# Output projection by token group with all sums formed ahead, residual copies behind the w2 loads, attention portions resized

## The chip, the cores and the metric

The kernel runs on one core of one Trainium2 chip. The metric is the device time of one execution in microseconds (us). It is about 1.7 us longer than the span in the profile, which counts from the first to the last instruction.

The engines are called as in the profile: PE is TensorE (PEld is its weight load), DVE is VectorE, ACT is ScalarE, POOL is GpSimd, SP is SyncE, which issues plain DMAs. "SPq" and "POOLq" are the sequencers that issue DMAs.

## The reference

One sequence of 2048 tokens, width 1024, bf16. A layer norm feeds two branches, and the result joins both with the input.

```python
xn = layernorm(x)
q, k, v = split(xn @ wqkv)                  # 32 heads of 32
# each token attends to 8 positions: itself and every second one before it
logits = q . k[pos - 2*w] * Dh**-0.5, w = 0..7      (masked where pos - 2*w < 0)
s = (softmax(logits) @ v[pos - 2*w]) @ wo            # output projection
g = silu((silu(xn @ w1) * (xn @ w3)) @ w2)           # MLP of inner width 3584
out = x + s * g
```

## The kernel before

Each large product is done with seven block products instead of eight, on two-by-two blocks of both factors: sums of blocks (s1 to s4 of the left factor, t1 to t4 of the right one) are formed on DVE, and products are accumulated in PSUM. For the output projection these are a11·b11, a12·b21, s1·t1, s2·t2, s3·t3, s4·b22 and a22·t4. A product is begun in one PSUM tile, copied by ACT to another where it serves as the start of a second chain, and finished by adding a stored partial result.

PE works through qkv (to about 160 us), the MLP's up and down parts of the first 1024 tokens and of the second, and a projection after each down part (about 505 and 700 us). The attention itself is work for DVE. It is cut in pieces that a generator hands out between the pieces of the foreground:

```python
def att_work():                       # cut: two chunks of 512 tokens at a time
    yield from scores(c, range(W))
    hooks.append(lambda: score_sums(c))
    yield STOP                        # ends the portion: the foreground runs the hook first
    exponents(c)
    yield 3.0                         # what the piece is booked at, in us of DVE
    yield from scores(c + 1, [0])
    weights(c)
    yield 2.5
    ...
PACE = (9, 8.8, 7.8, 8, 8.3)          # us of such work per step of the foreground, by stage
```

The projection goes product by product over two groups of 256 tokens (gp = 0, 1). s2 and s4 are formed in the middle of it:

```python
product(pa, a11, b11, True)                        # both groups
pb = [bank2(...) for gp in G2]
for gp in G2:
    act_copy(pb[gp][:], pa[gp][:])                 # ACT
with hp():
    nc.vector.tensor_sub(s2, s1, a11)
product(pa, a12, b21, False, finish(0, 0))         # needs pa free, so after the copy
with hp():
    nc.vector.tensor_sub(s4, a12, s2)
product(pe, s1, t1, True, ...)
product(pb, s2, t2, False, ...)
product(pb, s3, t3, False, finish(1, 1))
product(pe, s4, b22, False, finish(0, 1))
product(pb, a22, t4, False, finish(1, 0))
```

A finished piece s*g is not added to x by an engine. x was copied to the output beforehand (seven plain DMAs of 512 KB, issued between 25 and 35 us), and the piece is added to it by an accumulating DMA from POOL. Only the last 512 x 512 piece is done otherwise, with x loaded on the chip, an addition on DVE and a plain store by SP:

```python
def finished(b, u, dh, gp, ps, add):
    last = b == 1 and (u, dh) == (1, 0)
    ...
        if last:
            for i in I:
                ...
                nc.vector.tensor_add(g[:, i], g[:, i], xw[0][:, gp, i])
                nc.sync.dma_start(out=out_rows(...)[:, i], in_=g[:, i])
            return
        to_bf16(d, ps, add)
        anchor["v"] = nc.vector.tensor_mul(g, d, g)
        nc.gpsimd.dma_start(out=out_rows(out_flat, b, u, dh, gp), in_=g, accum_op=ALU.add)
```

While PE works on k, the weights of v ("wv") are loaded over a buffer that is just coming free, and their four sums are put into DVE's program as soon as the load is issued:

```python
def before_v(g):                  # called after the first and the second of k's two groups
    if g > 0:
        return
    for h in I:
        qkv_load(2, h, wv[h])
    tr(3)
    qkv_sums(*wv, sv)             # s1, s2, s4, s3 of wv
qkv_seven(1, 0, wk0, wk1, sk, before_v, snap[2:4])
```

Of the kernel before, what the change touches and what calls it, by code (L numbers as in the profile page):

```python
# [17 lines left out]
def kernel(  # L18
# [218 lines left out]

    def ln_dve(c, sts):
# [66 lines left out]

    def behind(key):
        return tc.issue_after(anchor[key].ins) if key in anchor else nullcontext()
# [182 lines left out]
    def att_work():  # L490
        for c in range(0, NC, 2):
# [5 lines left out]
            yield 3.0  # L497
            yield from scores(c + 1, [0])
            weights(c)
            yield 2.5  # L500
            yield from scores(c + 1, range(1, W))
            while c == 2 and "wo" not in state:
                yield STOP
            for n, t in enumerate(values(c)):
                yield t
                if n == 3:
                    hooks.append(lambda: score_sums(c + 1))
                    yield STOP
                    exponents(c + 1)
                    yield 3.0  # L510
                elif n == 7:
                    weights(c + 1)
                    yield 2.5
# [16 lines left out]
    PACE = (9, 8.8, 7.8, 8, 8.3)  # L530

    def bg(us):
# [5 lines left out]
        with priority(BG), behind("v"):  # L538
            while pace["credit"] > 0 and not hooks:
# [7 lines left out]
    def drain(c):  # L547
        n = 0
        while c not in state:
            bg(1)  # L550
            n += 1
        if n:
            print("drain", c, n)
# [66 lines left out]
    def mlp_up(b):  # L620
# [8 lines left out]
        for n, (g, fb) in enumerate(work):  # L629
# [32 lines left out]
            def e21(pb, f2=f2, hl=hl, n=n, fb=fb, h=h, g=g, both=both, last=last, m=m):  # L662
# [15 lines left out]
                if both and g == 0:  # L678
                    w2_step()
                    residual()  # L680
# [7 lines left out]
    def w2_load(fb):  # L688
        tiles["t", fb] = slot(4 + fb % 2, (2, 2, CH)) if fb < QB else r4(("t", fb), (2, 2, CH))
        nc.sync.dma_start(out=tiles["t", fb], in_=w2_q[:, fb])  # L690
# [148 lines left out]
    def wo_prepare(b):  # L839
# [5 lines left out]
        free = rows(0, 6)  # L845
        s1 = free[:, 0:4 * CH].bitcast(FP16).rearrange("p (j n) -> p j n", j=4)
        su2 = [free[:, (1 + gp) * 4 * CH:(2 + gp) * 4 * CH].bitcast(FP32).rearrange("p (i n) -> p i n", i=2) for gp in G2]
        a11, a12, a21, a22 = oT[:, 0, 0:4, :], oT[:, 0, 4:8, :], oT[:, 1, 0:4, :], oT[:, 1, 4:8, :]
        s2, s4, s3 = o16[:, 0, 0:4, :], o16[:, 0, 4:8, :], o16[:, 1, 0:4, :]

        wx[b] = (a11, a12, a21, a22, s1, s2, s3, s4), (b11, b12, b21, b22, t1, t2, t3, t4), su2
        with behind("v"):
            nc.vector.tensor_sub(t1, b12, b11)
            nc.vector.tensor_add(s1, a21, a22)
            nc.vector.tensor_sub(t2, b22, t1)
            nc.vector.tensor_sub(s3, a11, a21)
# [4 lines left out]
    def wo(b):  # L861
        def finish(u, dh, gp, ps, add=None):
            finished(b, u, dh, gp, ps, add)

        (a11, a12, a21, a22, s1, s2, s3, s4), (b11, b12, b21, b22, t1, t2, t3, t4), su2 = wx[b]

        def product(ps, lhs, rhs, first, after=None):
            run_hooks()
            for gp in G2:
                for i in I:  # L870
                    g = gp * 2 + i
                    mm(ps[gp][:, i], [lhs[:, j, g * P:(g + 1) * P] for j in range(4)], [rhs[:, j, :] for j in range(4)], first)
                if after is not None:
                    after(gp)

        pa = [bank2(f"wa{b}_{gp}") for gp in G2]
        product(pa, a11, b11, True)
        pb = [bank2(f"wb{b}_{gp}") for gp in G2]
        for gp in G2:
            act_copy(pb[gp][:], pa[gp][:])  # L880
        with hp():
            nc.vector.tensor_sub(s2, s1, a11)
        product(pa, a12, b21, False, lambda gp: finish(0, 0, gp, pa[gp]))
        with hp():
            nc.vector.tensor_sub(s4, a12, s2)
        pe = [bank2(f"we{b}_{gp}") for gp in G2]
        sp5 = [k4(f"wsp{b}_{gp}") for gp in G2]
        bg(7 * (1 - b))
        product(pe, s1, t1, True, lambda gp: act_copy(sp5[gp][:], pe[gp][:]))
        product(pb, s2, t2, False, lambda gp: act_copy(su2[gp], pb[gp][:]))  # L890
        bg(7 * (1 - b))
        product(pb, s3, t3, False, lambda gp: finish(1, 1, gp, pb[gp], sp5[gp][:]))
# [168 lines left out]
```

## Time and profile before

| what | us |
|---|---|
| median of the first 3 runs | 737.1 (736.4 to 737.7) |
| span of the profiled run | 732.3 |
| PE busy | 717.0 (98%) |
| DVE busy | 622.9 (85%) |
| last matmul to the end of the span | 7.0 |

The profile's page of the kernel before: the span, and busy time, share and instruction count of each engine.

```profile
span 732.3 us, 8789 instructions
...
PE 717.0 (98%) x3367; PEld 345.6 (47%) x3367; DVE 622.9 (85%) x676; ACT 314.2 (43%) x326; POOL 106.3 (15%) x161
```

PE bounds the kernel: only 15.3 us of the span are not PE time. A 128x512 matmul starts every 0.216 us, so a gap can be measured as the time from the start of one matmul to the start of the next, less 0.216 us. All gaps quoted below are computed so. The waits view names who ended PE's waits (us in total, times, longest); it counts from the modelled end of a matmul and so reads some 0.15 us lower.

```profile
PE wa L149 <- ACT wb L159: 1.6, 1, 1.6
PE aq L149 <- ACT bq L159: 1.5, 1, 1.5
...
PE bm L149 <- DVE wring L660: 0.8, 2, 0.5
```

These are three places: the first projection at 510 us (gap 1.81), the k products at 67 us (1.69), and two steps of the MLP at 310 and 335 us (0.68 and 0.65, the second in two steps of 0.48 and 0.17). What happened at 510 us is in the timeline of the kernel before (start us, us, engine, line, operation, out<-in, form, count, and in brackets the idle time before it with what ended it):

```profile
505.13 3.62 PE L149 MATMUL wa<-wring,oT 128*128 128x512 bf16 x16
...
507.12 1.22 DVE L438 TENSOR_TENSOR Es<-Es 128x1024 f32<-128x1024 f32 x1
...
508.37 1.06 ACT L440 ACTIVATE Es<-Es 128x1024 f32<-128x1024 f32 x1 [0.72 <-DVE Es L438]
...
509.33 1.91 ACT L159 COPY wb<-wa 128x1024 f32<-128x1024 f32 x2
...
510.39 1.45 PE L149 MATMUL wa<-wring,oT 128*128 128x512 bf16 x6 [1.65 <-ACT wb L159]
```

The copy of the first products to `wb` stood in ACT's order behind an exponential of the attention, which waited for DVE. PE had one product (16 matmuls for two groups) and then needed the copy.

At 67 us, the same view of the kernel before:

```profile
60.44 1.22 DVE L316 TENSOR_TENSOR wring<-wring 128x2048 f16<-128x2048 bf16 x1 [5.33 <-DMA wring<-in_A_wqkv_dram]
...
65.11 1.22 DVE L351 TENSOR_TENSOR pk<-eq,uq 128x1024 bf16<-128x1024 f32 x1
...
66.42 1.00 ACT L159 COPY bq<-aq 128x1024 f32<-128x1024 f32 x1 [6.28 <-DVE pk L351]
...
67.47 1.89 PE L149 MATMUL aq<-xT,wring 128*128 128x512 bf16 x8 [1.53 <-ACT bq L159]
```

DVE stands still for 5.33 us until wv has landed, then forms its four sums (L316 to L319), and only then does the addition L351 for k, whose PSUM tile ACT needs for its copy, for which PE waits.

The tail of the kernel before, in the same view: the last accumulating DMA is issued 0.7 us before PE's last matmul ends (725.31), and the last plain stores after it.

```profile
724.61 1.19 POOL L936 DMA_DIRECT2D out_dram<-h_sb  x1 [0.67 <-DVE h_sb L935]
...
725.20 3.19 SPq L932 DMA_DIRECT2D out_dram<-h_sb  x4
```

### The profile page before, as it was taken

The page shows a single profiled execution, that of the slowest core. Times are in us where ns is not written, and L with a number is a line of the kernel's source. Part 1 is how long each engine was busy: PE and PEld are TensorE (multiplying, and loading weights), DVE is VectorE, ACT ScalarE, POOL GpSimd, SP SyncE. Part 2 cuts the span into 40 slices and gives each one's busy share as a digit, 9 for nine tenths or more (in the row PEclk, how much of TensorE's full clock was granted, in tenths as well). Part 3 has the DMA queues.
Part 4 walks back from the last instruction along what each step waited for, and adds up shares of the span by engine and source line. Part 5 has one row for each costly group of instructions (what it writes and reads, how often), then busy time and mean ns, then how long its engine had stood idle before and what let it go on. Part 6 is the DMA issues. An engine that isn't in the chain of part 4 may idle for free.

```text
span 732.3 us, 8789 instructions
## 1 busy us (share of the span) xinstructions
PE 717.0 (98%) x3367; PEld 345.6 (47%) x3367; DVE 622.9 (85%) x676; ACT 314.2 (43%) x326; POOL 106.3 (15%) x161
## 2 busy tenths in 40 slices
PE   8999999999999999999999999999999999999996
PEld 4655665654444444444444444444444444444442
DVE  8996379886999886998999899959979899999535
ACT  5744343437654546654545411124364663121241
POOL 0000000010130110232302010010533032100012
PEclk9999999999999999999999999999999999999998
DMA  9899448864344343467756664559799364553525
GB/s 336 278 237 331 197 147 285 272 234 155 104 133 139 110 149 94 150 198 219 231 173 226 204 206 149 163 189 374 183 285 319 116 179 138 174 185 125 191 30 86
DMA packets 117577, 140.82 MB, mean 192 GB/s; under 512 B 14240, under 2 KB 91040, under 8 KB 116896
## 3 DMA queue, kind: packets, MB, share of 16 engines
q1 hardware_dynamic: 103408, 100.94, 44.2%
q0 software_dynamic: 14128, 39.33, 17.8%
q8 instruction: 26, 0.43, 0.2%
q14 instruction: 15, 0.12, 0.1%
HBM read 98.30 MB, written 39.32 MB: 188 GB/s over the span
## 4 chain that ended last, share of the span: by engine, by line
PE 83%; DVE 11%; DMA 2%; ACT 1%; issue 1%; SPq 0%; DVEq 0%; ACTq 0%
PE bm L149 17%; PE em L149 11%; PE am L149 11%; PE db L149 10%; PE bq L149 7%; PE de L149 7%; PE da L149 7%; PE eq L149 4%; PE aq L149 4%; PE wb L149 2%; PE wa L149 2%; DMA wring<-in_A_wqkv_dram 2%; PE we L149 1%; DVE BC L465 1%; DVE stats L246 1%
## 5 line engine op out<-in xcount | busy, mean ns | idle before, releaser
L149 PEld LDWEIGHTS <-wring 128*128 128x128 f16 (+1 forms) x1920 | 201.6, 105 | 217.9 <-issue 6.8
L149 PEld LDWEIGHTS <-h_sb 128*128 128x128 f16 (+1 forms) x1024 | 107.8, 106 | 113.7 <-DVE xs L291 1.0
L149 PE MATMUL bm<-xs,wring 128*128 128x512 f16 x504 | 117.4, 379 | 0.1
L149 PE MATMUL am<-xT,wring 128*128 128x512 bf16 x336 | 79.9, 379 | 0.1
L410 DVE TENSOR_TENSOR pt<-qt,kT 128x4096 bf16<-128x4096 bf16 x32 | 73.2, 2289 | 0.6
L149 PE MATMUL db<-wring,h_sb 128*128 128x512 f16 x336 | 73.2, 379 | 0.0
L465 DVE TENSOR_TENSOR BC<-Ep,vT 128x2048 bf16<-128x2048 bf16 x56 | 66.9, 1219 | 0.2
L647 ACT ACTIVATE g<-um 128x1024 bf16<-128x1024 f32 x28 | 29.6, 1057 | 52.6 <-DVE um L645 52.6
L645 DVE TENSOR_TENSOR um<-em,um 128x1024 f32<-128x1024 f32 x28 | 34.2, 1221 | 20.9 <-PE em L149 20.9
L451 POOL DMA_DIRECT2D Ep<-pb x64 | 37.9, 623 | 90.4 <-DVE pb L447 35.9
L149 PE MATMUL da<-wring,h_sb 128*128 128x512 bf16 x224 | 49.0, 379 | 0.0
L149 PE MATMUL bm<-h_sb,wring 128*128 128x512 f16 x168 | 40.2, 379 | 0.9 <-DVE wring L660 0.8
L149 PE MATMUL em<-xs,wring 128*128 128x512 f16 x168 | 39.7, 379 | 0.0
L149 PE MATMUL em<-xT,wring 128*128 128x512 bf16 x168 | 39.7, 379 | 0.0
L475 DVE TENSOR_TENSOR oT<-oT,BC 128x2048 bf16<-128x2048 bf16 x32 | 39.1, 1220 | 0.4
L412 DVE TENSOR_TENSOR pt<-pt 128x2048 bf16<-128x2048 bf16 x32 | 39.0, 1219 | 0.4
L159 ACT COPY pm<-em 128x1024 f32<-128x1024 f32 x28 | 28.4, 1013 | 22.7 <-PE em L149 22.7
L159 ACT COPY bm<-am 128x1024 f32<-128x1024 f32 x28 | 28.0, 998 | 21.1 <-PE am L149 20.8
L159 ACT COPY um<-bm 128x1024 f32<-128x1024 f32 x28 | 28.3, 1012 | 18.3 <-PE bm L149 17.9
L666 ACT CAST g<-bm 128x1024 bf16<-128x1024 f32 x28 | 28.3, 1011 | 17.3 <-PE bm L149 17.3
L351 DVE TENSOR_TENSOR pk<-eq,uq 128x1024 bf16<-128x1024 f32 x12 | 14.7, 1222 | 21.3 <-PE eq L149 12.1
L936 POOL DMA_DIRECT2D out_dram<-h_sb x14 | 16.9, 1283 | 98.6 <-DVE h_sb L935 97.9
(172 smaller groups left out, 983.5 us busy)
## 6 DMA issues: line engine op xcount, KB each, us to landing
wring<-in_B_w_dram SPq DMA_DIRECT2D x61, 512.0 KB, 4.4
wring<-t_dram SPq DMA_DIRECT2D x16, 512.0 KB, 5.4
t_dram<-wring POOLq DMA_DIRECT2D x14, 512.0 KB, 3.6
wring<-in_A_wqkv_dram SPq DMA_DIRECT2D x6, 1024.0 KB, 7.6
wring<-t_dram SPq DMA_DIRECT2D x16, 384.0 KB, 5.5
wring<-in_B_w_dram SPq DMA_DIRECT2D x12, 384.0 KB, 4.3
wring<-in_A_x_dram SPq DMA_DIRECT2D x16, 256.0 KB, 5.1
Ep<-pb POOLq DMA_DIRECT2D x64, 64.0 KB, 4.2
```

The costliest lines, as they stand in the source:

```text
L149: anchor["pe"] = nc.tensor.matmul(ps, lhsT=lhs[k], rhs=rhs[k], start=(first and k == 0), stop=(k == n - 1), skip_group_check=not first,)
L159: nc.scalar.copy(out=out_, in_=in_)
L351: anchor["v"] = nc.vector.tensor_add(d, ps[:], a[0][:])
L410: nc.vector.tensor_mul(p_t[:], q[:], kT[:, :, o:o + CH])
L412: nc.vector.tensor_add(p_t[:, 0:4, :], p_t[:, 0:4, :], p_t[:, 4:8, :])
L451: nc.gpsimd.dma_start(out=pr[c][r:P:NR, :, sq * P:(sq + 1) * P], in_=pb[sq * 32:(sq + 1) * 32, :, :])
L465: nc.vector.tensor_mul(dst, E[:, w, :].unsqueeze(1).to_broadcast([P, n, CH]), vT[:, js, o:o + CH])
L475: nc.vector.tensor_add(A, A, B if w0 else C)
L645: v = nc.vector.tensor_add(su2[:], pe[:], su2[:])
L647: nc.scalar.activation(out=hl["g"][:, :, CH:], in_=su2[:], func=ACTF.Silu)
L666: nc.scalar.copy(out=hl["g"][:, :, 0:CH], in_=pb[:])
L936: nc.gpsimd.dma_start(out=out_rows(out_flat, b, u, dh, gp), in_=g, accum_op=ALU.add)
```

## The change

There are three parts. The intent of the first (A) is that no product of the projection should wait for a copy or a sum: the work goes by token group, so that other products lie between the first use of a PSUM tile and its second, and s2 and s4 are formed in the preparation. With it the direct finish at the end shrinks from 512 to 256 tokens, each half of which is treated separately. The second part (B) takes the 512 KB copies out of the busy start and puts them behind the w2 loads. The third part (C) cuts the attention into portions whose booked sizes are closer to what DVE takes, so that foreground additions on DVE come in time.

Part A, cut to its core:

```diff
 def wo_prepare(b):
     ...
+            nc.vector.tensor_sub(s2, s1, a11)
+            nc.vector.tensor_sub(s4, a12, s2)
 def wo(b):
-        product(pa, a11, b11, True)              # over both groups, and so on
-        ...
+        if b == 1:
+            xw[0] = k4("xw", (2, CH), BF16)
+            nc.sync.dma_start(out=xw[0], in_=out_rows(x_flat, 1, 1, 0, 1))
+        for gp in G2:
+            last = b == 1 and gp == 1
+            product(both(pa), gp, a11, b11, True)
+            product(both(pe), gp, s1, t1, True)
+            flush()                              # the last product of the group before
+            act_copy(pb[:], pa[:])               # in halves where last
+            act_copy(sp5[:], pe[:])
+            bg((7, 0)[gp] * (1 - b))
+            product(pbs, gp, s2, t2, False)
+            act_copy(su2[:], pb[:])              # in halves where last
+            product(both(pe), gp, s4, b22, False)
+            finished(b, 0, 1, gp, pe, su2[:])
+            product(pbs, gp, s3, t3, False)
+            finished(b, 1, 1, gp, pb, sp5[:])
+            product(both(pa), gp, a12, b21, False)
+            finished(b, 0, 0, gp, pa)
+            def tail(...):
+                product(pbs, gp, a22, t4, False)
+                finished(b, 1, 0, gp, pb)
+            pend.append(tail)
 def finished(b, u, dh, gp, ps, add=None):
-        last = b == 1 and (u, dh) == (1, 0)
+        last = (b, u, dh, gp) == (1, 1, 0, 1)
```

Part B:

```diff
 def w2_load(fb):
-        nc.sync.dma_start(out=tiles["t", fb], in_=w2_q[:, fb])
+        anchor["sp"] = nc.sync.dma_start(out=tiles["t", fb], in_=w2_q[:, fb])
 def residual():
-        ...copy of one block...
+        if copies:
+            r0, n, dh = copies.pop(0)
+            with behind("sp"):
+                nc.sync.dma_start(out=out_flat[r0:r0 + n, ...], in_=x_flat[r0:r0 + n, ...])
 # in the step of the MLP's up part
                 if both and g == 0:
                     w2_step()
+                if both:
                     residual()
+    copies.insert(0, (3 * CH, 2 * P, 0))         # an eighth copy, for the smaller direct finish
```

Part C:

```diff
             exponents(c)
-            yield 3.0
+            yield 2.8
             yield from scores(c + 1, [0])
             weights(c)
-            yield 2.5
+            yield 3.7
             ...
+            todo = [3.7, 2.8]
+            at = 0
             for n, t in enumerate(values(c)):
                 yield t
                 if n == 3:
                     hooks.append(lambda: score_sums(c + 1))
-                    yield STOP
-                    exponents(c + 1)
-                    yield 3.0
-                elif n == 7:
-                    weights(c + 1)
-                    yield 2.5
+                elif n > 3 and not hooks and todo and n > at:
+                    at = n + 3
+                    (exponents if len(todo) == 2 else weights)(c + 1)
+                    yield todo.pop()
-    PACE = (9, 8.8, 7.8, 8, 8.3)
+    PACE = (9.5, 9.2, 7.3, 8.2, 8.6)
-            while pace["credit"] > 0 and not hooks:
+            while pace["credit"] > 0:
 # drain() also runs the hooks
```

More of the change, by code (lines that the diff above doesn't have):

```diff
@@ L236, in x_load, with behind @@
             nc.sync.dma_start(out=xt[c][:, st, :], in_=x_flat[g * P:(g + 1) * P, :])
+    def behind(key):
+        return tc.issue_after(anchor[key].ins) if key in anchor else nullcontext()
     def ln_dve(c, sts):
@@ L302 @@
     B0 = B_of(xT[:, 0], xT[:, 1], xT[:, 2], xs)
-    def behind(key):
-        return tc.issue_after(anchor[key].ins) if key in anchor else nullcontext()
     def qkv_sums(w0, w1_, st):
@@ L549, in drain @@
         while c not in state:
+            run_hooks()
             bg(1)
@@ L844, in wo_prepare @@
         t4 = r4("wo", (4, CH), FP16)
-        free = rows(0, 6)
-        s1 = free[:, 0:4 * CH].bitcast(FP16).rearrange("p (j n) -> p j n", j=4)
-        su2 = [free[:, (1 + gp) * 4 * CH:(2 + gp) * 4 * CH].bitcast(FP32).rearrange("p (i n) -> p i n", i=2) for gp in G2]
+        s1, s2, s4 = [rows(2 * i, 2, FP16).rearrange("p (j n) -> p j n", j=4) for i in range(3)]
         a11, a12, a21, a22 = oT[:, 0, 0:4, :], oT[:, 0, 4:8, :], oT[:, 1, 0:4, :], oT[:, 1, 4:8, :]
-        s2, s4, s3 = o16[:, 0, 0:4, :], o16[:, 0, 4:8, :], o16[:, 1, 0:4, :]
-        wx[b] = (a11, a12, a21, a22, s1, s2, s3, s4), (b11, b12, b21, b22, t1, t2, t3, t4), su2
+        s3 = o16[:, 1, 0:4, :]
+        wx[b] = (a11, a12, a21, a22, s1, s2, s3, s4), (b11, b12, b21, b22, t1, t2, t3, t4)
         with behind("v"):
@@ L861, in wo @@
     def wo(b):
-        def finish(u, dh, gp, ps, add=None):
-            finished(b, u, dh, gp, ps, add)
-        (a11, a12, a21, a22, s1, s2, s3, s4), (b11, b12, b21, b22, t1, t2, t3, t4), su2 = wx[b]
-        def product(ps, lhs, rhs, first, after=None):
-            run_hooks()
-            for gp in G2:
-                for i in I:
-                    g = gp * 2 + i
-                    mm(ps[gp][:, i], [lhs[:, j, g * P:(g + 1) * P] for j in range(4)], [rhs[:, j, :] for j in range(4)], first)
-                if after is not None:
-                    after(gp)
@@ L876, in wo @@
-        pa = [bank2(f"wa{b}_{gp}") for gp in G2]
-        product(pa, a11, b11, True)
-        pb = [bank2(f"wb{b}_{gp}") for gp in G2]
-        for gp in G2:
-            act_copy(pb[gp][:], pa[gp][:])
-        with hp():
-            nc.vector.tensor_sub(s2, s1, a11)
-        product(pa, a12, b21, False, lambda gp: finish(0, 0, gp, pa[gp]))
-        with hp():
-            nc.vector.tensor_sub(s4, a12, s2)
-        pe = [bank2(f"we{b}_{gp}") for gp in G2]
-        sp5 = [k4(f"wsp{b}_{gp}") for gp in G2]
@@ L888, in wo @@
-        bg(7 * (1 - b))
-        product(pe, s1, t1, True, lambda gp: act_copy(sp5[gp][:], pe[gp][:]))
-        product(pb, s2, t2, False, lambda gp: act_copy(su2[gp], pb[gp][:]))
-        bg(7 * (1 - b))
-        product(pb, s3, t3, False, lambda gp: finish(1, 1, gp, pb[gp], sp5[gp][:]))
-        product(pe, s4, b22, False, lambda gp: finish(0, 1, gp, pe[gp], su2[gp]))
-        product(pb, a22, t4, False, lambda gp: finish(1, 0, gp, pb[gp]))
+        (a11, a12, a21, a22, s1, s2, s3, s4), (b11, b12, b21, b22, t1, t2, t3, t4) = wx[b]
@@ new lines, in wo, with product, tail @@
+        if b == 1:
+            xw[0] = k4("xw", (2, CH), BF16)
+            nc.sync.dma_start(out=xw[0], in_=out_rows(x_flat, 1, 1, 0, 1))
+        def product(ps, gp, lhs, rhs, first):
+            for i in I:
+                g = gp * 2 + i
+                mm(ps[i], [lhs[:, j, g * P:(g + 1) * P] for j in range(4)], [rhs[:, j, :] for j in range(4)], first)
+        both = lambda t: [t[:, i] for i in I]
+        for gp in G2:
+            run_hooks()
+            last = b == 1 and gp == 1
+            pa = bank2(f"wa{b}_{gp}")
+            product(both(pa), gp, a11, b11, True)
+            pe = bank2(f"we{b}_{gp}")
+            product(both(pe), gp, s1, t1, True)
+            flush()
+            pb = [bank2(f"wb{b}_{gp}{i}")[:, i] for i in I] if last else bank2(f"wb{b}_{gp}")
+            for i in I:
+                if last:
+                    act_copy(pb[i], pa[:, i])
+            if not last:
+                act_copy(pb[:], pa[:])
+            pbs = pb if last else both(pb)
+            sp5, su2 = k4(f"wsp{b}_{gp}"), k4(f"wsu{b}_{gp}")
+            act_copy(sp5[:], pe[:])
+            bg((7, 0)[gp] * (1 - b))
+            product(pbs, gp, s2, t2, False)
+            for i in I:
+                if last:
+                    act_copy(su2[:, i], pb[i])
+            if not last:
+                act_copy(su2[:], pb[:])
[5 more added lines that the diff above has]
+            finished(b, 0, 0, gp, pa)
+            def tail(gp=gp, pb=pb, pbs=pbs):
+                product(pbs, gp, a22, t4, False)
+                finished(b, 1, 0, gp, pb)
+            pend.append(tail)
@@ L895, in wo @@
+        flush()
         release("wo")
@@ L903, in to_bf16 @@
             nc.scalar.copy(out=d, in_=ps[:])
+        elif isinstance(ps, list):
+            for i in I:
+                nc.vector.tensor_add(d[:, i], ps[i], add[:, i])
         else:
@@ L907, with finished @@
     xw = {}
-    copies = [(b, u, dh) for b in I for u, dh in ((0, 0), (1, 1), (0, 1), (1, 0)) if (b, u, dh) != (1, 1, 0)]
+    copies = [((2 * b + u) * CH, CH, dh) for b in I for u, dh in ((0, 0), (1, 1), (0, 1), (1, 0)) if (b, u, dh) != (1, 1, 0)]
+    copies.insert(0, (3 * CH, 2 * P, 0))
     def residual():
-        b, u, dh = copies.pop(0)
-        r0 = (2 * b + u) * CH
-        nc.sync.dma_start(out=out_flat[r0:r0 + CH, dh * CH:(dh + 1) * CH], in_=x_flat[r0:r0 + CH, dh * CH:(dh + 1) * CH])
-    def finished(b, u, dh, gp, ps, add):
-        last = b == 1 and (u, dh) == (1, 0)
-        if last and gp == 0:
-            xw[0] = k4("xw", (2, 2, CH), BF16)
-            for i in I:
-                nc.sync.dma_start(out=xw[0][:, i], in_=out_rows(x_flat, b, u, dh, i))
+        if copies:
+            r0, n, dh = copies.pop(0)
+            with behind("sp"):
+                nc.sync.dma_start(out=out_flat[r0:r0 + n, dh * CH:(dh + 1) * CH], in_=x_flat[r0:r0 + n, dh * CH:(dh + 1) * CH])
+    def finished(b, u, dh, gp, ps, add=None):
+        last = (b, u, dh, gp) == (1, 1, 0, 1)
         g = g_tile(b, u, dh, gp)
@@ L927, in finished @@
                 for i in I:
-                    if gp == 0:
-                        nc.scalar.copy(out=d[:, i], in_=ps[:, i])
-                    nc.vector.tensor_mul(g[:, i], d[:, i] if gp == 0 else ps[:, i], g[:, i])
-                    nc.vector.tensor_add(g[:, i], g[:, i], xw[0][:, gp, i])
+                    nc.vector.tensor_mul(g[:, i], ps[i], g[:, i])
+                    nc.vector.tensor_add(g[:, i], g[:, i], xw[0][:, i])
                     nc.sync.dma_start(out=out_rows(out_flat, b, u, dh, gp)[:, i], in_=g[:, i])
```

## The prediction

> **What bounds the kernel.** TensorE. The page gives PE 717.0 us busy of a 732.3 us span at full clock. In the timeline a 128x512 matmul starts every 0.216 us (8 take 1.73 us), and some 3,300 of that form make nearly all of it; the change removes none. So at most 15 us can be had. PE idle time (PE timeline; releasers from the waits view):
> - 0 to 12 us, first loads and transposes: about 7 us, not touched.
> - 28.9, 38.4, 47.0 us: 0.7, 0.3, 0.2 us, DVE.
> - 67.5 us: 1.7 us, ACT copy behind DVE, behind the wv load (issued 48.8, landed about 60.4).
> - 310.4 and 335.1 us: 0.7 and 0.65 us, DVE late (window 300-400: DVE 93%).
> - 510.4 us: 1.8 us, "PE wa <- ACT wb": the copy of the first products waited behind an Exp, itself behind DVE.
> - Tail: last matmul ends 725.3, span 732.3: 7.0 us.
>
> **The change, costed.**
> 1. Projection by token group. A copy (1.0 us, ACT) now has 5 us and more of other products before the second use of its source, where it had 1.7. s2 and s4 (1.23 us each, DVE) move into the preparation, where DVE has room (30.8 busy of 40 us in 660-700). The 1.8 us at 510 should vanish. PSUM rotation looks safe: the tightest reuse has 1.73 us of products over a 1.2 us copy; in the last group I estimate a wait of 0.2 us.
> 2. The x-to-out copies (7 x 512 KB, issued 25.3 to 34.5 us, DMA 80 to 100% busy until 40 us) move behind the MLP's w2 loads, about 170 to 230 us, where DMA is 30 to 60% busy. The Trainium skill ("Trainium Kernel Development and Optimization", Key Constraints) says all issuing queues share the same 16 DMA engines; the trace agrees in that q writes were late beside the copies (DVE pk <- DMA q_dram, 2.9 us). But they had landed by 42 us, and the wv load is released by PE only at 48.7, so the 1.7 us at 67.5 should mostly stay. Gain 0.4 us.
> 3. Portions. Summing DVE durations between successive "bm" additions in issue order (12.1 us of PE each): before it swings 6 to 14 us, with 14.0 ahead of the 310 us gap; after, mostly 8 to 13. The 1.3 us at 310/335 should vanish. The second attention half ends later, near 694 us; its sums follow by about 702, in time.
> 4. Tail. After: last DVE operation an estimated 2.1 us after the last matmul (2.5 now), but the last accumulating POOL DMA is issued at +0.75 us instead of -0.7. These took 4.5 to 6.0 us to land, the plain SP one 3.4. The accumulate becomes the last arrival; the tail stays 6.5 to 7.6 us: no gain.
>
> **Sum.** 1.8 + 0.4 + 1.3 - 0.5 (new waits) + 0 (tail) = 3.0 us, all PE idle time on the critical path. Predicted 734.0 us, range 731.3 to 736.8. Faster by over 2% (below 722.3): 1%; within 2%: 97%; slower by over 2%: 2%.
>
> **What would show each step.** (1) no PE gap over 0.3 us in either projection; (2) DMA busy falls in 25-42 us, the q-write wait goes, the 67.5 us gap persists; (3) gaps at 310/335 us gone, PE busy still 717 us; (4) the last landing is an accumulate, last matmul to end of span about 7 us.
>
> **What would make it wrong.** The 67.5 us gap going too: 1.7 us more. A new DVE or ACT lateness around an Exp, or at the second projection (attention unfinished): several us less. Copies delaying weight loads at 170 to 230 us.

## The result, and the profile after

| | before | after |
|---|---|---|
| median, 6 runs each (us) | 736.2 (735.0 to 737.7) | 736.4 (734.5 to 737.6) |
| ratio, after over before | | 1.000 (95%: 0.998 to 1.002) |
| span of the profiled run | 732.3 | 735.9 |
| last matmul to the end | 7.0 | 8.8 |

A ratio here is the mean time of one kernel's fast runs over the mean of the other's of the same rounds, so it is not quite the ratio of the medians that stand beside it. The profiled run of the changed kernel happened to be one of its slower ones; a second profile of the same kernel had a span of 733.4 us. All outputs are right.

The page of the kernel after:

```profile
span 735.9 us, 8786 instructions
...
PE 718.5 (98%) x3367; PEld 345.9 (47%) x3367; DVE 622.3 (85%) x674; ACT 314.1 (43%) x327; POOL 103.2 (14%) x162
```

As predicted, the work on each engine has hardly changed. The waits of PE in the kernel after:

```profile
PE aq L149 <- ACT bq L159: 2.6, 1, 2.6
...
PE am L149 <- ACT bm L159: 0.7, 1, 0.7
...
PE zp L425 <- DVE dsu L822: 0.5, 1, 0.5
...
PE bm L149 <- DVE h_sb L661: 0.2, 1, 0.2
```

The 1.6 us at the projection and the 0.8 us of the MLP are gone. The wait at 67 us is there still, larger here, and three new ones have come. The timeline of the kernel after at the projection shows what part A meant to do. The copy still waits for its place, but it ends while PE is busy with s1·t1 and with the last product of the group before:

```profile
508.17 1.89 PE L149 MATMUL wa<-wring,oT 128*128 128x512 bf16 x8
...
510.15 1.00 ACT L159 COPY wb<-wa 128x1024 f32<-128x1024 f32 x1 [0.76 <-PE wa L149]
...
511.62 1.89 PE L149 MATMUL wb<-h_sb 128*128 128x512 f16 x8
```

One new wait is at 178 to 184 us, in the same view of the kernel after:

```profile
176.97 1.22 DVE L438 TENSOR_TENSOR Es<-Es 128x1024 f32<-128x1024 f32 x1
178.10 1.22 DVE L646 TENSOR_TENSOR um<-em,um 128x1024 f32<-128x1024 f32 x1
178.22 1.06 ACT L440 ACTIVATE Es<-Es 128x1024 f32<-128x1024 f32 x1 [2.46 <-DVE Es L438]
...
179.24 1.21 DVE L661 TENSOR_TENSOR h_sb<-bm,pm 128x1024 bf16<-128x1024 f32 x1
179.29 1.28 ACT L648 ACT_TABLE_LOAD   x1
...
180.59 1.06 ACT L648 ACTIVATE g<-um 128x1024 bf16<-128x1024 f32 x1
...
181.55 1.01 ACT L159 COPY bm<-am 128x1024 f32<-128x1024 f32 x1
...
182.61 1.89 PE L149 MATMUL am<-h_sb,wring 128*128 128x512 bf16 x8 [0.65 <-ACT bm L159]
```

The exponential (L440), which with the old portions fell at 183 and 508 us, now falls at 178 and 514 us, and the first of these is between a late DVE addition and the ACT copy that PE needs: behind the exponential ACT still has a table load and an activation to do before the copy. From the start of the exponential to the matmul that waits for the copy it is 4.39 or 4.40 us in all nine profiles with the new portions. So a collision like that at 510 us has come to an MLP step.

The tail of the kernel after:

```profile
726.86 0.68 DVE L951 TENSOR_TENSOR h_sb<-h_sb 128x1024 bf16<-128x1024 bf16 x1
...
727.84 1.18 POOL L952 DMA_DIRECT2D out_dram<-h_sb  x1 [0.49 <-DVE h_sb L951]
727.94 1.37 SPq L948 DMA_DIRECT2D out_dram<-h_sb  x2
```

The last accumulating DMA is now issued 0.77 us after the last matmul's end (727.07). By the trace's record of DMA completions it landed at 734.19, 6.35 us after its issue; the last plain store landed at 733.85. POOL's closing drain ended at 735.10, and the span at 735.88.

A ledger of the places that differ, in two profiles of each kernel (gap of PE in us; the tail is from the last matmul's end to the end of the span):

| place | before | before, again | after | after, again |
|---|---|---|---|---|
| 310 and 335 us, MLP | 1.33 | 1.33 | 0 | 0 |
| 510 to 516 us, first projection | 1.81 | 1.92 | 0.22 | 0.22 |
| 178 to 186 us, MLP | 0.22 | 0.43 | 1.21 | 1.05 |
| 489 us, MLP, score sums | 0 | 0 | 0.64 | 0.65 |
| 581 us, MLP | 0 | 0 | 0.24 | 0.23 |
| tail | 6.99 | 6.50 | 8.81 | 8.55 |
| sum of these | 10.35 | 10.18 | 11.12 | 10.70 |
| 67 us, k | 1.69 | 2.20 | 2.80 | 1.96 |
| half-rate matmuls after it | 0 | 0 | 1.65 | 0 |

The gains are there: 1.33 and, on average, 1.87 - 0.22 = 1.65 us, together 2.98. Against them stand 0.80 us more at 178 us, 0.65 at 489, 0.24 at 581 and 1.93 in the tail, together 3.6. The last two lines belong to both kernels and vary from run to run; they are most of why the first profile of the kernel after looks 3.6 us longer, and the experiments below look into them.

### The profile page after: what moved, and what is told of

It is laid out like the page before. It is cut to its first block, busy times and chain, and to the rows that moved or that the text cites. A ratio compares the mean times of both kernels' runs of the same rounds, so it can differ in the third digit from the quotient of the medians.

```text
span 735.9 us, 8786 instructions
## 1 busy us (share of the span) xinstructions
PE 718.5 (98%) x3367; PEld 345.9 (47%) x3367; DVE 622.3 (85%) x674; ACT 314.1 (43%) x327; POOL 103.2 (14%) x162
## 4 chain that ended last, share of the span: by engine, by line
PE 57%; DVE 19%; issue 14%; DMA 4%; ACT 3%; POOL 2%; POOLq 0%; SPq 0%; DVEq 0%; ACTq 0%
PE bm L149 16%; PE am L149 11%; PE em L149 11%; PE bq L149 6%; DVE pt L410 4%; PE aq L149 4%; PE eq L149 4%; DVE pt L412 2%; DMA wring<-in_A_wqkv_dram 2%; PE db L149 2%; DVE stats L249 1%; DMA t_dram<-wring 1%; PE wb L149 1%; DVE pt L414 1%; POOL out_dram L952 1%
## 5 line engine op out<-in xcount | busy, mean ns | idle before, releaser
L149 PEld LDWEIGHTS <-h_sb 128*128 128x128 f16 (+1 forms) x1088 | 114.1, 105 | 122.1 <-issue 1.7
L952 POOL DMA_DIRECT2D out_dram<-h_sb x15 | 18.8, 1387 | 97.9 <-DVE h_sb L951 97.7
```

The source lines that it names most:

```text
L149: anchor["pe"] = nc.tensor.matmul(ps, lhsT=lhs[k], rhs=rhs[k], start=(first and k == 0), stop=(k == n - 1), skip_group_check=not first,)
```

## The experiments

The theory after the result: the change gains what it was meant to gain, and gives it back in the tail (an accumulating DMA as last arrival) and in new DVE and ACT collisions; the gap at 67 us is untouched and makes the spread. The first rival: part C alone removes the gap at 510 us, since it moves the exponential away from there, and part A gains nothing. The second rival: the copies at their new place disturb the MLP or the loads, and so cost what A and C gain. The third: the tail is longer because DVE's last work became longer, not because of the accumulating DMA. The runs were made in three groups; the kernels of a group share a chip and 11 runs of the kernel before, with medians 736.25, 735.62 and 735.07 us.

### before_again: the kernel before, unchanged

> The kernel before, unchanged, as a second look: how far do two profiles and two timings of the same kernel differ? Theory A (the two differences that are not local to the change are chance): the PE gap near 67 us, 1.7 us in the first profile of before, varies from execution to execution, by a us or more, with the landing of the wv load; the PE gaps elsewhere (0.7 at 310, 0.6 at 335, 1.8 at 510) and the tail (last matmul to end of span, 7.0 us) repeat within 0.3 us. Ratio 1.000 +- 0.002. Rival B: the gap near 67 us is 1.7 us every time in this kernel, and the 2.8 us with eight half-rate matmuls in the profile of after came from the change.

Measured: 734.98 us, ratio 0.9986 (0.9965 to 1.0008), span 732.8. The gap at 67 us was 2.20 us this time, so it does vary without the change. The tail was 6.50 us, 0.49 less than in the first profile, where 0.3 had been expected at most. The same kernel against itself so shows how fine a ratio can be read: about 0.2%.

### port_only: part C alone

```diff
+ part C of the change, all of it; parts A and B left out
```

> Attention portions alone (pace figures, no stop of the background work at a hook). Theory A: gaps at 310 and 335 us gone (-1.3 us), new ones near 182 us (+1.2) and 490 us (+0.6) as in after; the 1.8 us gap at 510 us (copy behind the Exp in the first projection) stays, since only the reorder of the projection removes it; tail 7.0 us. Sum +0.5 us, ratio about 1.001. Rival: the portions also move the Exp away from the projection, so the gap at 510 us goes with this part alone.

Measured: 736.56 us, ratio 1.0005 (0.9983 to 1.0028). The gaps at 310 and 335 us are gone, as in the kernel after, and 489 us has its new gap of 0.65. But the first projection still waits, 1.88 us, in the waits view of this run:

```profile
PE wa L149 <- ACT wb L159: 1.7, 1, 1.7
```

So the first rival falls: it is part A that removes the gap at 510 us. Part C also brought a gap of 0.55 us at 180 us, about half of the 1.2 that had been expected, and one of 1.22 us at 685 us, at ACT, which the whole change does not have; with that at 489 us these eat up its 1.33 us. Its tail is 6.36 us, short as before.

### copy_only: part B alone

```diff
+ anchor["sp"] = nc.sync.dma_start(out=tiles["t", fb], in_=w2_q[:, fb])
  def residual():
+     if not copies:
+         return
      b, u, dh = copies.pop(0)
+     with behind("sp"):
          nc.sync.dma_start(...)              # the same seven copies
  # in the step of the up part: residual() for every step with both, as in part B
```

> x-to-out copies behind the w2 loads, alone. Theory A: DMA quiet from 28 to 36 us, but every PE gap as in before: 310, 335, 510 us and a tail of 7.0 us; gap near 67 us within the spread of the kernel before; ratio 1.000. Rival B: the copies were harmless where they were, and their move makes the gap near 67 us longer (2.6 us or more, with half-rate matmuls after it): +1 to +2.8 us.

Measured: 735.35 us, ratio 0.9994 (0.9972 to 1.0016). The copies did move. The busy view by stretch (stretch, its length, busy us and count of PE, PEld, DVE, ACT and POOL, granted clock, DMA share, GB/s), first of the kernel before, then of this run:

```profile
26.00:40.00 14.00, 13.31 (x61) 7.36 (x60) 13.91 (x21) 8.04 (x11) 0.00 (x0) 1.00 0.97 319
160.00:230.00 70.00, 69.83 (x329) 31.77 (x328) 59.90 (x77) 39.54 (x39) 12.43 (x22) 1.00 0.44 141
```

```profile
26.00:40.00 14.00, 13.36 (x61) 7.41 (x61) 13.92 (x21) 7.94 (x10) 0.00 (x0) 1.00 0.19 70
160.00:230.00 70.00, 69.35 (x323) 32.04 (x327) 59.36 (x75) 39.04 (x39) 13.50 (x23) 1.00 0.59 187
```

The DMA share falls from 0.97 to 0.19 in the first stretch, where PE and DVE are as busy as before, and rises from 0.44 to 0.59 in the second, again without a loss. The gaps at 38 and 47 us, which I had put down to the copies, stay at 0.3 and 0.17 us. The gap at 67 us was 2.40 us, without half-rate matmuls after it. So part B is worth nothing that these runs can show, in either direction, and the second rival falls. This profile has a gap of 0.97 us at 149 us, behind a late write of v. `proj_only`, where the copies are early, has the same gap (0.88 at 151 us, behind a write of v too), so it is not a mark of the late copies.

### proj_only: part A alone

```diff
+ part A of the change, all of it
  def residual():                             # copies at their old place, eight of them
-     b, u, dh = copies.pop(0)
+     for r0, n, dh in [copies.pop(0) for i in range(2 if len(copies) == 8 else 1)]:
          nc.sync.dma_start(...)
```

> Output projection by token group alone. Theory A: the 1.8 us gap at 510 us shrinks to 0.3 us or less; the tail grows from 7.0 to 8.8 us, since the last accumulating DMA is issued 0.75 us after the last matmul instead of 0.7 us before it, takes about 6 us to land, and the POOL queue drains only then; gaps at 310 and 335 us stay. Sum about 0: ratio 1.000. Rival: the long tail of after was a slow DMA in one execution; then the tail here is 7 to 7.6 us and the ratio 0.998.

Measured: 738.81 us, ratio 1.0035 (1.0015 to 1.0055): slower, and clearly so. The gap at 510 us is down to 0.22, but a new one of 1.34 us stands at the end of the same projection. The timeline of this run:

```profile
527.85 1.23 DVE L447 TENSOR_TENSOR pb<-Es 128x1024 bf16<-128x1024 f32 x1
...
531.46 1.22 DVE L923 TENSOR_TENSOR h_sb<-wb,wsp 128x1024 bf16<-128x1024 f32 x1
...
532.73 1.45 PE L149 MATMUL wb<-wring,oT 128*128 128x512 f16 x6 [1.17 <-DVE h_sb L923]
```

The last product, a22·t4, goes into the PSUM tile that the addition L923 has to read first. With the old portions a row of attention work (to 529.1 us) stands before the additions of this projection on DVE. The tail is 8.34 us. So A and C are not independent: A makes the projection need DVE at another moment, and C is what keeps DVE free then. The new gap alone does not make this run slower than before: at the projection 1.6 us are won and 1.34 lost, and about 1.6 us go in the tail. That is half of the 2.6 us that the ratio stands for. This profile also has gaps of 0.60 at 131 and 0.88 at 151 us, and half-rate matmuls (1.63 us), none of them at a place of part A; how much of the loss is theirs is not known.

### proj_port: parts A and C, with the copies early

```diff
+ parts A and C of the change
  copies at their old place, as in proj_only
```

> Projection reorder and portions together, copies left where they were (after minus the copies). Theory: the 1.34 us gap at 532.7 us of the projection alone came because the old portions put attention work (pt 2.28 us, weights 1.2 us) ahead of the addition that the last product waits for; with the new portions it is gone, as in after; gaps near 180 (1.2) and 489 (0.65) us and a tail of 8.2 to 8.8 us stay; ratio 1.000 to 1.002 like after. Rival (the copies' move carries part of the gain of after): 1.003 like the projection alone.

Measured: 736.09 us, ratio 1.0025 (1.0000 to 1.0050). No gap at 532 us; gaps at 180 us (1.17 in all), 489 us (0.64) and 581 us (0.23) as in the kernel after; tail 7.83 us, a little less than expected. In the profile the kernel after without part B behaves as the kernel after. The ratio does not decide it: 1.0025 is nearer to the rival's 1.003 than to 1.002, and its interval holds both. The pair of best versions below compares the two places of the copies again.

### after_again: the kernel after, unchanged

> The changed kernel once more. If the ledger of local gaps is right, the gaps at 180.5 (0.4), 182.6 (0.8) and 490.9 (0.64) us and a tail of 8.3 to 8.8 us come back in this profile, and 310, 335 and 510 us are free of gaps. The gap near 67 us comes back with 1.7 to 2.8 us, and the half-rate matmuls after it may or may not (they came with 2.17 and 2.80 us and did not with 1.69, 2.08, 2.20, 2.40). Ratio to before 1.000 to 1.002. Rival (the copies or the change made that gap longer): 2.6 us or more again, with half-rate matmuls.

Measured: 736.56 us, ratio 1.0002 (0.9969 to 1.0035), span 733.4, tail 8.55 us. The result is confirmed, and so is the ledger, this time without half-rate matmuls.

### tail_direct: the second to last piece finished on DVE

The tail was tested by taking the accumulating DMA away from the end. The piece (1,0,0,gp 1), the last one that POOL adds, is finished as the very last one is: x loaded beforehand into a free part of `h_sb`, one more addition on DVE (0.68 us), a plain store.

```diff
+ xw[1] = h_sb[:, 26:28, 0:CH]
+ nc.sync.dma_start(out=xw[1], in_=out_rows(x_flat, 1, 0, 0, 1))
  ...
  anchor["v"] = nc.vector.tensor_mul(g, d, g)
+ if (b, u, dh, gp) == (1, 0, 0, 1):
+     nc.vector.tensor_add(g, g, xw[1])
+     nc.sync.dma_start(out=out_rows(out_flat, b, u, dh, gp), in_=g)
+     return
+ # and these rows are left out of the copies
```

> After, but the last accumulate (u=0, dh=0 of the last token group) is done as x loaded early, one more DVE addition and a plain store on SP. Theory: the tail of after is the landing of that accumulate and the drain of the POOL queue behind it: the last POOL issue now lands about 4 us after the last matmul, the last SP store is issued at about +2.8 us and lands 3.4 us later: tail 7.0 to 7.4 us, -1.5 us; ratio to before 0.998 to 0.999. Rival: the tail is the length of the DVE chain and the stores themselves; then the extra DVE addition (0.69 us) makes it 8.8 to 9.5.

Measured: 735.22 us, ratio 0.9985 (0.9955 to 1.0016) over before. The timeline of its tail; the last matmul ended at 726.63:

```profile
727.35 0.68 DVE L956 TENSOR_TENSOR h_sb<-h_sb 128x1024 bf16<-128x1024 bf16 x1
...
728.06 0.38 SPq L957 DMA_DIRECT2D out_dram<-h_sb  x1
...
729.12 0.34 SPq L951 DMA_DIRECT2D out_dram<-h_sb  x1
```

The tail is 6.71 us instead of 8.81 and 8.55, although DVE works longer after the last matmul (it ends 2.5 us after it; 1.85 us in the kernel after). So the third rival falls, and the accumulating DMA was what held the end. Two things make it dear. It lands late: from 720 us on in the kernel after, the view of DMA issues (count, KB each, median us from issue to landing) says

```profile
out_dram<-h_sb POOLq DMA_DIRECT2D x4, 256.0 KB, 4.8
out_dram<-h_sb SPq DMA_DIRECT2D x2, 128.0 KB, 4.2
```

and the very last took 6.35, 6.10, 5.89, 5.72 and 5.38 us in the five profiles that have it at the end. And what follows a landing is longer: POOL's drain ended 0.87 to 0.92 us after the last accumulating DMA had landed in all of these, and also in the kernel before (730.65, 731.52) and in `tail_direct` (landed 731.01, drain ended 731.88, where it no longer mattered), while SP's drain ended 0.15 us after the last plain store there (732.38, 732.53). From the last landing to the end of the span it is 1.69 us in the kernel after, where an accumulating DMA comes last, and 0.96 in `tail_direct`, where a plain one does. This run changes the accumulation and the issuing queue in one step, so which of the two makes the DMA dear is not shown.

The longer drain is not new, though. In the kernel before, POOL's drain ended at 731.52 and SP's at 731.53; in its second profile POOL's was the later one (732.03 against 731.88), and both times the end came 1.65 us after the last accumulating DMA had landed. So what the change added to the tail, 1.82 us in the first pair of profiles and 2.05 in the second, is the later issue (0.77 us after the last matmul instead of 0.70 before it: 1.47 us) and the slower landing (6.35 instead of 6.04 us, and 6.10 instead of 5.55).

The ratio of this run to before has an interval that holds 1, so the 1.9 us are shown by the trace more than by the times. The profiled run had half-rate matmuls, too.

### wv_late2: the sums of wv later in DVE's order

This tests the gap at 67 us. The four sums of wv are put behind the additions of k's second group.

```diff
  def before_v(g):
      if g > 0:
+         qkv_sums(*wv, sv, True)
          return
      ...
      tr(3)
-     qkv_sums(*wv, sv)
  def qkv_sums(w0, w1_, st, late=False):
+     with behind("u") if late else nullcontext():      # s1 behind the last addition but one
          nc.vector.tensor_add(s1, a21, a22)
+     with behind("v") if late else nullcontext():      # the others behind the last addition
          nc.vector.tensor_sub(s2, s1, a11)
          nc.vector.tensor_sub(s4, a12, s2)
          nc.vector.tensor_sub(s3, a11, a21)
```

> After, but the sums of the wv weights stand on DVE behind the k additions that free the PSUM tile (only s1 before the last of them). Theory: the gap near 67 us is head-of-line blocking on DVE: the addition pk<-eq (1.2 us), whose inputs are ready at 60.6 us, waits behind four sums (4.6 us) that wait for wv. With the order turned round the gap shrinks from 1.7-2.8 us to under 0.7 us and no half-rate matmuls follow: -1.5 to -4 us, ratio to before about 0.996. Rival: the gap is the landing of wv itself; then it stays at 1 us or more (PE then waits for s1).

Measured: 734.41 us (733.21 to 734.72), ratio 0.9973 (0.9939 to 1.0006) over before. The gap at 67 us is gone; 0.30 us at 64.8 is left, where PE waits for s1. First a line of the timeline of the kernel after, then the timeline of this run:

```profile
61.36 1.23 DVE L316 TENSOR_TENSOR wring<-wring 128x2048 f16<-128x2048 bf16 x1 [6.43 <-DMA wring<-in_A_wqkv_dram]
```

```profile
62.35 1.23 DVE L353 TENSOR_TENSOR pk<-eq,uq 128x1024 bf16<-128x1024 f32 x1 [6.82 <-DMA k_dram<-pk]
...
63.49 1.22 DVE L317 TENSOR_TENSOR wring<-wring 128x2048 f16<-128x2048 bf16 x1
...
64.67 1.00 ACT L159 COPY bq<-aq 128x1024 f32<-128x1024 f32 x1 [4.11 <-PE aq L149]
```

The addition for k (L353 here) no longer stands behind the sums. It now starts when an earlier write of k has landed (62.23 us) and its buffer is free, and ACT's copy waits for PE and no longer for DVE. The Trainium skill ("TensorE: Matmul & The Clock Gate", Part 1, architectural detail) says that "ACT/DVE are strict FIFO", and this agrees: nothing but the place in the order was changed, and a gap of 1.96 to 2.80 us became 0.30. In nine profiles without this mend the gap is DVE's wait for wv less 3.63 or 3.64 us: 5.33 and 1.69 in the kernel before, 6.43 and 2.80 in the kernel after, 5.59 and 1.96 in its repeat, and likewise in the other six. The gap is thus set by when wv lands (60.4 to 61.4 us, from a load issued at about 49), and that varies from run to run.

What follows the gap varies more. In the kernel after, of which this is the timeline, 8 matmuls took 3.02 us where 8 take 1.89 before:

```profile
68.38 3.02 PE L149 MATMUL aq<-xT,wring 128*128 128x512 bf16 x8 [2.63 <-ACT bq L159]
```

Eight matmuls there, beginning with the fourth, started every 0.427 us instead of 0.216, which costs 1.65 us. The same eight came in `proj_only` (gap 2.16) and `tail_direct` (2.57); they did not come after gaps of 1.69, 1.96, 2.02, 2.08, 2.20 and 2.40 us. The Trainium skill (same page, Part 1, "What's actually happening") tells of a clock gate that halves PE's clock after an idle window of about 3.4 us, in windows that run freely, so that the number of matmuls at half rate is "run-variable". The traces agree with the half rate, with its length (eight times 0.427 is 3.4 us) and with the free windows; but here gaps of 2.2 to 2.8 us were enough.

The trace's own record of the granted clock shows what decides. In the kernel after it says half from 68.99 to 72.40 us, which is 3.41 us, and in all 14 profiles every change of the clock lies on a grid of 3.413 us, which starts at another moment in each run. So what counts is not the gap but how much of it falls into one window of that grid. After windows with 2.17 (`proj_only`), 2.57 (`tail_direct`), 2.80 (the kernel after) and 3.41 us (`best_y60`, below) of idle PE the next window was at half clock. Between 20 and 720 us no other window of the 14 profiles has more than 2.08 us of idle PE, and none of them was followed by half clock. The gap of 2.40 us in `copy_only` lay across two windows, with at most 1.83 us in one.

Whether the gap makes the spread of the times is not shown. The six times of this run lie within 1.5 us of each other, and the five of `before_wv`, with the same mend, within 1.2, where the 11 of the kernel before are spread over 3.7, 7.4 and 3.7 us in the three groups. But the six of `tail_direct`, without the mend, lie within 1.5 us too, and those of the combined version below, with it, are spread over 4.1.

### after_tail_wv, best_early_copies and before_wv: putting it together

```diff
  after_tail_wv      = the whole change + tail_direct + wv_late2
  best_early_copies  = parts A and C + tail_direct + wv_late2, copies at their old place
  before_wv          = the kernel before + wv_late2
```

> Both mends on after. If the two are independent the gains add: -3 to -5 us on after, ratio to before about 0.994 to 0.997, 731 to 733 us in the timed runs, with a narrower spread than the 3.5 us of before, since the gap whose length varies is gone. Rival (what is won at 67 us is given back later, DVE being 85% busy): gain of the tail alone, ratio 0.998.

Measured: 733.17 us (731.26 to 735.40), ratio 0.9957 (0.9924 to 0.9990), span 729.7, tail 6.64, gap at 64 us 0.14. The gains add up as expected; the narrower spread did not come.

> The kernel with both mends (last accumulate replaced, wv sums later on DVE), but x-to-out copies early as in before. Theory: the place of the copies is worth nothing: same time as with the copies late (0.9957 of before, profile span 729.7), within 0.2%; DMA busy in 26 to 40 us but no new PE gap. Rival: with the gap at 67 us mended the early copies show up as late landings of the q writes: +1 us.

Measured: 731.37 us (730.62 to 732.11), ratio 0.9955 (0.9939 to 0.9971), span 730.4, tail 6.87, gap at 65 us 0.93, at s1 again, which here comes late behind an addition that starts at 62.79 us. A gap of the rival's size is thus in the profile, but the time is not longer. On the same chip `proj_port`, without the two mends, took 736.09 us.

> The kernel before with the wv sums later on DVE and nothing else. Theory: gap near 67 us 1.7-2.2 us -> 0.3 us, everything else as in before (310, 335, 510 us, tail 6.5 to 7.0): -1.5 to -2 us, ratio 0.997, no half-rate matmuls, spread of the timed runs narrower than before's 3.5 us or more. Rival (the spread comes from elsewhere): same gain but the same spread.

Measured: 732.58 us (731.65 to 732.87, five runs), ratio 0.9970 (0.9953 to 0.9987), span 730.8, gap at 65 us 0.55.

The two mends take the changed kernel to 0.43% below the kernel before, wherever the copies stand: both orders give the same ratio within 0.02%, each against before on its own chip. It is within the 2% that count as the same, but the intervals are clear of 1. Two thirds of it come from the mend at wv, which needs no change of the projection at all: `before_wv` is 0.30% below before. What is left for A, C and the direct finish together is about 0.15%, or 1 us of 735, taken as the difference of the two ratios, whose intervals overlap. `best_early_copies` and `before_wv` can also be compared directly, since they share a chip: the means of their six and five runs are 731.4 and 732.5 us, 1.1 us apart, with a standard error of 0.3.

### best_y60: a try at the collision at 178 us

The first new gap was to be mended by booking the exponential at 6.0 us instead of 2.8, so that less background work is put ahead of the foreground there.

```diff
  # on after_tail_wv
             exponents(c)
-            yield 2.8
+            yield 6.0
             yield from scores(c + 1, [0])
```

> Both mends, and the first exponents of a pair counted at 6.0 us instead of 2.8, so that less attention work goes into the same portion. Theory: the gaps near 176 and 178 us (0.28 and 0.82) are DVE 1.1 us late with the um addition (two small attention operations stand before it); they shrink by about 0.9 us in sum; ratio about 0.9945. Rival: the ACT queue, where the Exp and two table loads stand before the copy, holds the gap at 178 us as it is.

Measured: 737.98 us (736.87 to 741.20), ratio 1.0052 (1.0031 to 1.0073). It failed twice. The gap at 178 us grew, to 1.46 us, so my idea of that place was wrong. The rival names the mechanism, ACT's order, though not that the gap would grow: from the start of the exponential to the matmul behind the copy it is 4.39 us here too, as in the kernel after. The exponential began 2.93 us before PE wanted the copy, in the kernel after 3.58 us. And the attention was not finished when the second projection began, which cost 4.02 us there, in the timeline of this run:

```profile
702.92 1.23 DVE L477 TENSOR_TENSOR oT<-oT,BC 128x2048 bf16<-128x2048 bf16 x1
704.18 1.23 DVE L856 TENSOR_TENSOR h_sb<-oT 128x2048 f16<-128x2048 bf16 x1
...
705.46 3.43 PE L149 MATMUL we<-h_sb 128*128 128x512 f16 x8 [3.86 <-DVE h_sb L856]
```

The last attention value (L477) is done only at 704 us, the sum s1 that needs it after that, and PE waits for s1. Here, too, eight matmuls after the gap ran at half rate. So 3.2 us more on each booking leave no room for DVE to finish; the paces of part C are near a limit on this side, and the new gaps at 178 and 489 us stay unmended.

## Why the prediction was right or wrong

The time on record was 734.0 us with a range of 731.3 to 736.8, and 97% for "within 2%". The kernel after took 736.4 us, a ratio of 1.000. The range held and the class was right, but that says little: a kernel without any gain (736.2 us, the kernel before) lies in the range too. The gain of 3.0 us was not there, because two terms of the sum were mis-sized, one was not there, and the others were right. A part of the distance to 734.0 is the base: the three runs of before that were known then had a median of 737.1, six have 736.2.

1. *"The 1.8 us at 510 should vanish."* Right. 1.81 and 1.92 us became 0.22. It takes part A to do it: part C alone left 1.88 us. What I had not seen is that part A alone would wait for the additions at 532 us (1.34 us) and be slower than before.
2. *"Gain 0.4 us"* for the copies. Wrong, it was 0: `copy_only` and the pair of best versions both say so. I had read waits of DVE for writes of q, 2.9 us in all, as a sign that these writes were late beside the copies; the trace does not bear it out. Those waits lie at 148 and 159 us in the kernel before (0.98 and 1.94 us), when the copies had long landed, and the kernel after has one of 3.4 us at 151 us. A total in the waits view has no time beside it; the timeline would have told. The page cited there (the Trainium skill, "Trainium Kernel Development and Optimization", Key Constraints) is not contradicted: the DMA engines were 97% busy from 26 to 40 us. But nothing on the path was waiting for them. That the gap at 67 us would persist was right.
3. *"The 1.3 us at 310/335 should vanish."* Right, in every profile with part C but that of `best_y60`, which changed the portions again (0.39 at 311 us). Mis-sized was the end of the attention: not near 694 us but at 700.7. Its sum s1 was done at 703.0, 1.4 us before PE needed it, so it was in time with less room than I thought.
4. *"- 0.5 (new waits)."* The mechanism was right ("a new DVE or ACT lateness around an Exp"), the size was not: 0.80 more at 178 us, 0.65 at 489 and 0.24 at 581, together 1.69 us. Counting DVE time between the foreground additions did not show where ACT's exponential would land between two copies.
5. *"The tail stays 6.5 to 7.6 us: no gain."* Wrong: 8.81 and 8.55, a loss of 1.93 us on average. The issue at +0.75 us was right to 0.02, and so was that the accumulate would be the last arrival. What failed is the time behind it. I took 4.5 to 6.0 us for its landing, and the last one of before (6.04) was the one to go by: it was 6.35 and 6.10. And I left out that what follows the landing is 0.73 us longer for an accumulating DMA (1.69 against 0.96), which the kernel before had already paid (1.65). `tail_direct` gives these 2 us back.

The sum with the measured terms, from the ledger: 1.65 + 0 + 1.33 - 1.69 - 1.93 = -0.64 us, a loss of 0.1%. The measured ratios of 1.000 and 1.0002 agree with it within their intervals.

Whether early or late copies shift the landing of wv looked open in the nine profiles: DVE's waits for it average 5.67 us with early copies and 6.07 with late ones, and the ranges overlap. Over all 14 profiles, the second half of wv takes 11.66 us from issue to landing with early copies (11.1 to 12.4) and 11.74 with late ones (11.4 to 12.2), so no shift is to be seen. Three things stay open: whether the accumulation or the issue from POOL makes the last DMA dear, why the exponential came later, as PE counts, when it was booked dearer, and what spreads the times.

## What to carry to other kernels

On an engine that works in order, look for the first instruction that waits for a load and at what stands behind it: moving four sums behind two additions gained more here than a reordered projection. Before a change is credited with the gaps that it closes, go through the last arrivals one by one, with the time from issue to landing and from landing to the end for each kind of DMA, since an accumulating DMA that was issued 1.47 us later cost 1.9 us here. And where foreground and background work share an engine, test the parts of a change together as well as alone: the new order lost time with the old portions, and the new portions gained nothing with the old order.

## What the Trainium skill lacked or had wrong

- "TensorE: Matmul & The Clock Gate", Part 1, puts the half rate after an idle window of about 3.4 us. Here the windows are there, 3.41 us long, but one need not be idle throughout: half rate followed windows with 2.17, 2.57, 2.80 and 3.41 us of idle PE, and none with 2.08 us or less. The loss was 1.5 to 1.7 us each time.
- "DMA: Bandwidth & Descriptors", Anatomy of one DMA, gives 2.0 us plus bytes at 436 KB per us for a DMA from GpSimd, from which an estimate for 256 KB is 2.6 us. The accumulating DMAs of 256 KB at the end of this kernel took 4.8 us in the median and 6.35 us at most, with others under way beside them; no accumulating DMA took under 4.0 us in any of the 14 profiles. The page says that accumulation goes through GpSimd only (SWDGE vs HWDGE vs iDMA), but not what it costs.
- "Runtime: NRT & Kernel Launch", The ~15µs preamble/postamble breakdown, lists what follows a kernel as fixed stages. No page says that it depends on which kind of DMA lands last. Here POOL's drain ended 0.87 to 0.92 us after the last accumulating DMA had landed, SP's drain 0.15 us after its last plain store, and the end of the span came 1.65 to 1.69 us after the first landing where POOL's drain held it (the kernel after, and the second profile of the one before), 0.96 us after the second in `tail_direct`.
